# One machine model with turns at SBUF and TensorE's clock windows sets the order of issue of a clustered attention and feed-forward kernel

## The chip, the cores and the metric

The kernel runs on one core of a Trainium2 chip. The metric is device time in microseconds (us). Three runs before the change took 917.51, 917.72 and 917.95 us, a median of 917.72. The profiled execution took 917.96 us. The engines are named as in the profile: PE (TensorE's matmuls), PEld (its weight loads), DVE (VectorE), ACT (ScalarE), POOL (GpSimd) and SP (SyncE, which issues the DMAs).

## The reference

Attention over 4 batches, 8 heads, 768 positions and 64 dimensions, in which a query sees only the keys of its own cluster (of 16); then a feed-forward layer of width 2048 with a piecewise quadratic gate. All is float32.

```python
q_assign = np.argmax(np.einsum('bhsd,hcd->bhsc', q_n, c_n), axis=-1)
k_assign = np.argmax(np.einsum('bhsd,hcd->bhsc', k_n, c_n), axis=-1)
mask = q_assign[:, :, :, None] == k_assign[:, :, None, :]
scores = scale * np.matmul(q, k.transpose(0, 1, 3, 2))
scores = np.where(mask, scores, -1000000000.0)
scores = scores - np.max(scores, axis=-1, keepdims=True)
attn = np.exp(scores)
attn = attn / (np.sum(attn, axis=-1, keepdims=True) + 1e-09)
attn_out = np.matmul(attn, v)
x = attn_out.transpose(0, 2, 1, 3).reshape(B * S, H * D)
h = x @ w_in
g = np.where(h >= 1, h, np.where(h <= -1, 0.0, (h + 1) ** 2 / 4))
out = g @ w_out
```

## The kernel before

Float32 operands are split into a high and a low float16 part, and a product is three matmuls (high by high, high by low, low by high). Heads go in pairs, four pairs in a batch. Queries go in chunks of 256, three chunks in a batch, so there are twelve **units** (a batch and a chunk); for a unit each pair of heads has four score tiles of 128 queries by 768 keys.

A score tile runs so: PE multiplies into a PSUM bank; DVE takes the minimum along a row and copies to SBUF (`sS`, with `sbi`; a custom operation that the order's rows call ISA); ACT takes the exponential; ACT casts the high half (`hl`) and POOL subtracts for the low half; a transposing DMA on SP's queue brings it to `pT`. In the first steps every other tile is transposed on PE instead, ACT casts and DVE subtracts (`pT<-bank`). Then PE multiplies by `v` into `banka`, ACT and DVE scale (`rb`), and ACT and POOL split the result into `x`.

The feed-forward layer of a unit is eight pairs of products. The first product goes into a half bank; DVE clamps (`r`), ACT squares, DVE takes the gate (`r` again), ACT casts (`g`), POOL subtracts, and the second product adds into `bank2`.

The work of preparation lies in the start, and a part of it at each change of batch: for a pair of heads the splits of k and q (`n`, in the first batch also `x`, `g`, `o`) and of v (`kvq<-kvq,sv`), the assignment to clusters (`mx`, `bank`, `has`, `er`) and a product of k by `phi`; a reduction over v (`v_am`); and, once only, sixteen pieces of the weights, each with an absolute value on ACT, a shift on DVE (`wk<-wk`), a merge of bits on DVE (`w<-w,wk`), a sign on ACT, a multiplication on POOL, a scaling and a cast on ACT and a subtraction on POOL (`w<-w`), with small reductions (`w_am`, `w_iw`, `w_sw`). `ffn_scale` makes the scales of the feed-forward layer by sixteen small instructions on DVE.

No engine call issues at once. A `Recorder` keeps each as a node with its engine, its cost in ns (`price`, line 76), what it reads and writes, and the step at which the program asks for it; a group of matmuls is one node. There are 3634. `issue` (line 276) then plans. `forward` goes through time and lets each engine take, from the nodes that are ready, the one of best priority; `backward` does the same from the end and so gives new priorities; after `ROUNDS` the order of the shortest planned span is issued, at one line (291), so all rows of the profile have that line. Each engine runs its instructions in the issued order.

In `price`, a DVE operation of the kind that can wait for POOL at SBUF costs a flat 400 ns more:

```python
wide = [a for a in ins if self.free(a) > 1 or n == 1]
wait = 400 if not ps and (len(wide) > 1 or op in ("tensor_scalar", "tensor_copy")) else 0
```

In `forward`, a matmul costs twice as much before 75 us of planned time (`COLD`) and its plain cost after it.

Of the kernel before, what the change touches and what calls it, by code (L numbers as in the profile page):

```python
# [27 lines left out]


LATENCY = dict(tensor=280, scalar=252, vector=230, gpsimd=175)  # L30
COLD, AHEAD = 75e3, 1500

LOOK, MARGIN = 0.4, 4000
ROUNDS = 8

class Recorder:
# [37 lines left out]
    def price(self, eng, op, out, ins, kw):  # L76

        if "dma" in op:
            n = 1
            for k in out.shape:  # L80
                n *= k
            kb = n * mybir.dt.size(out.dtype) / 1024

            return 33, 79.0 if kb == 2 else kb, "transpose" in op
        n = max(self.free(a) for a in [out] + ins[:1])
        ps = any(a.space == PSUM for a in ins)
        cols = sum(isinstance(kw.get(k), bass.AP) for k in ("scale", "bias", "scalar", "scalar1", "scalar2"))
        if eng == "tensor":
            n = self.free(ins[1])
            half = self.free(ins[0]) <= 64 and n > 100  # L90
            if ins[1].dtype == F32:
                n *= 4

            return n / 4.8 + 9 if half else max(n / 2.4 + 2.5, 24)
        if eng == "scalar":
            cols += kw.get("accum_out") is not None
            first = n == 1 and kw.get("scale") == 0.0
            return 93 + n / 1.2 + 94 * cols - 43 * ps + 1283 * first
        if eng == "vector":
            wide = [a for a in ins if self.free(a) > 1 or n == 1]  # L100
            wait = 400 if not ps and (len(wide) > 1 or op in ("tensor_scalar", "tensor_copy")) else 0
            fast = 1
            if op in ("tensor_scalar", "tensor_copy") and not ps:
                fast = 4 if mybir.dt.size(out.dtype) == 2 and mybir.dt.size(ins[0].dtype) == 2 and n > 64 else 2
            return 68 + n / 0.96 / fast + 61 * cols + 20 * (op == "reciprocal") + wait
        return 55 + n * (2.03 if op == "tensor_tensor" else 0.9 if op == "memset" else 3.5)

    def group(self):
        return Group(self)

    def add(self, eng, op, fn, args, kw):
        outs = [kw[k] for k in ("out", "accum_out") if kw.get(k) is not None]
        pos = [a for a in args if isinstance(a, bass.AP)]
        if "out" not in kw:
            outs.insert(0, pos.pop(0))
        ins = pos + [a for k, a in kw.items() if k not in ("out", "accum_out") and isinstance(a, bass.AP)]
        node = self.open
        if node is None:
            node = Node(eng, self.step, len(self.nodes))
            self.nodes.append(node)  # L120
        assert node.eng == eng
        p = self.price(eng, op, outs[0], ins, kw)
        if isinstance(p, tuple):
            node.cost += p[0]
            node.dma = p[1:]
        else:
            node.cost += p
        node.calls.append((fn, args, kw))
        for aps, w in ((ins, False), (outs, True)):
            for ap in aps:  # L130
                name, parts = self.regions(ap)
                for r in parts:
                    self.touch(node, name, r, w)
                    if ap.space == PSUM:
                        node.banks.update((name, x) for x in range(r[2] // 2048, (r[3] - 1) // 2048 + 1))

    def touch(self, node, name, r, w):
# [12 lines left out]
        keep.append((r, w, node))  # L150
        self.seen[name] = keep

    def forward(self, prio):

        clock, ready, avail = {}, {}, {}
        left = {x: len(x.preds) for x in self.nodes}
        at = dict.fromkeys(self.nodes, 0.0)
        for x in self.nodes:
            if not x.preds:
                heappush(ready.setdefault(x.eng, []), (0.0, prio[x], x.i))  # L160
        hw, ring, sent, span = 450.0, 0.0, [], 0.0
        self.order, bank = [], {}
        todo = len(self.nodes)
        while todo:
            todo -= 1
            best = None
            for e, q in ready.items():
                now = clock.get(e, 0.0)
# [7 lines left out]
            t, e = best  # L176
# [8 lines left out]
            if more:  # L185
# [2 lines left out]
                q.remove((t, prio[self.nodes[i]], i))  # L188
                heapify(q)
                x = self.nodes[i]  # L190

            free = max((until for k in x.banks for o, until in bank.get(k, {}).items() if o != e), default=0.0)
            if free > t:
                clock[e] = t
                heappush(q, (free, prio[x], x.i))
                todo += 1
                continue
            if x.dma and x.dma[0] > 256 and ring > t + AHEAD:

                clock[e] = t  # L200
                heappush(q, (ring - AHEAD, prio[x], x.i))
                todo += 1
                continue
            if x.dma:
                kb, tr = x.dma
                t = max(t, hw, sent[-8] if len(sent) > 7 else 0.0)
                clock[e] = t + x.cost
                hw = t + (650 if tr else 475)
                ring = max(ring, hw + (650 if tr else 784)) + kb * (5.6 if tr else 3.25)
                if tr:  # L210

                    hw = max(hw, ring - 1000)
                end = ring + (400 if tr else 1300)
                sent.append(end)
            else:
                clock[e] = t + x.cost * (2 if e == "tensor" and t < COLD else 1)
                end = clock[e] + LATENCY[e]
            for k in x.banks:
                bank.setdefault(k, {})[e] = end
            x.start, x.busy = t, clock[e]  # L220
            span = max(span, end)
            self.order.append(x)
            for y in x.succs:
                raw = x.dma or x.eng != y.eng or (y.preds[x] and x.eng != "tensor")
                at[y] = max(at[y], end if raw else x.busy)
                left[y] -= 1
                if not left[y]:
                    heappush(ready.setdefault(y.eng, []), (at[y], prio[y], y.i))
        return span

    def backward(self, prio):

# [6 lines left out]
        for _ in self.nodes:  # L239
# [19 lines left out]
                clock[e] = t + kb * (5.6 if tr else 3.25)  # L259
                start[x] = -clock[e] - 1275  # L260
            else:
                clock[e] = t + x.cost
                start[x] = -clock[e]
            for p, raw in x.preds.items():
                lag = 0.0
# [10 lines left out]
    def issue(self):  # L276
# [3 lines left out]
        prio = {x: x.step for x in self.nodes}  # L280
        best = None
        for _ in range(ROUNDS):
            span = self.forward(prio)
            if best is None or span < best[0]:
                best = span, self.order
            prio = self.backward({x: x.start for x in self.nodes})
        span, self.order = best
        with self.tc.manual_schedule():
            for x in self.order:
# [1 line left out]
                    fn(*args, **kw)  # L291


class Node:
    def __init__(self, eng, step, i):
        self.eng, self.step, self.i = eng, step, i
        self.banks = set()
        self.cost, self.dma, self.calls, self.preds, self.succs = 0.0, None, [], {}, []


# [825 lines left out]
```

## Time and profile before

| | |
|---|---|
| Median of three runs | 917.72 us |
| Profiled execution | 917.96 us, span 916.2 us |
| Busy PE, PEld | 819.7, 566.2 us |
| Busy DVE, ACT, POOL | 621.8, 660.5, 580.4 us |
| Mean granted clock of TensorE | 0.961 |
| Idle DVE before a score reduction, for PE | 68.2 us |
| Idle POOL before `hl`, for ACT | 122.1 us |

A row of a group gives line, engine, operation, output and inputs by the program's names, shapes and count; then the busy time, the mean of one in ns, and the idle time of the engine before them with what ended it. A row of a stretch gives its bounds and length, the busy time of each engine with the number of instructions, the granted clock, the share of the DMA engines and GB/s. A row of the timeline gives the start, the duration, and the instruction. A row of waits gives who waited for whom, the sum, the times and the longest.

### The profile page before, as it was taken

The page shows a single profiled execution, that of the slowest core. Times are in us where ns is not written, and L with a number is a line of the kernel's source. Part 1 is how long each engine was busy: PE and PEld are TensorE (multiplying, and loading weights), DVE is VectorE, ACT ScalarE, POOL GpSimd, SP SyncE. Part 2 cuts the span into 40 slices and gives each one's busy share as a digit, 9 for nine tenths or more (in the row PEclk, how much of TensorE's full clock was granted, in tenths as well). Part 3 has the DMA queues.
Part 4 walks back from the last instruction along what each step waited for, and adds up shares of the span by engine and source line. Part 5 has one row for each costly group of instructions (what it writes and reads, how often), then busy time and mean ns, then how long its engine had stood idle before and what let it go on. Part 6 is the DMA issues. An engine that isn't in the chain of part 4 may idle for free.

```text
span 916.2 us, 19559 instructions
## 1 busy us (share of the span) xinstructions
PE 819.7 (89%) x7462; PEld 566.2 (62%) x7462; DVE 621.8 (68%) x1335; ACT 660.5 (72%) x1145; POOL 580.4 (63%) x521
## 2 busy tenths in 40 slices
PE   2556669899998999999998999999998999999998
PEld 2344446556765766776666666666665666667664
DVE  6999987887796665556987665557868555444232
ACT  5778999979767587778676687678766677776232
POOL 1369888986764667766575677656565666666322
PEclk9756779999999999999999999999999999999999
DMA  9989675658998878868899968878998866666100
GB/s 312 238 204 189 133 208 129 152 120 183 185 201 166 161 141 164 156 147 187 166 205 167 176 124 163 157 155 195 178 196 149 149 132 127 111 121 110 30 24 24
DMA packets 403263, 142.82 MB, mean 156 GB/s; under 512 B 380000, under 2 KB 395360, under 8 KB 403168
## 3 DMA queue, kind: packets, MB, share of 16 engines
q1 hardware_dynamic: 403168, 141.56, 76.3%
q8 instruction: 58, 0.95, 0.4%
q14 instruction: 37, 0.30, 0.1%
HBM read 40.40 MB, written 6.29 MB: 51 GB/s over the span
## 4 chain that ended last, share of the span: by engine, by line
PE 68%; DVE 14%; issue 4%; ACT 2%; POOL 2%; ACTq 0%; DVEq 0%; POOLq 0%
PE bank L291 51%; PE banka L291 10%; PE bankh L291 8%; DVE sS L291 3%; DVE r L291 2%; DVE bank L291 2%; DVE kvq L291 2%; DVE n L291 1%; POOL hl L291 1%; DVE w L291 1%; ACT sS L291 1%; DVE mx L291 1%; ACT hl L291 0%; ACT wk L291 0%; DVE bankh L291 0%
## 5 line engine op out<-in xcount | busy, mean ns | idle before, releaser
L291 POOL TENSOR_TENSOR hl<-sS,hl 128x768 f16<-128x768 f32 x181 | 311.4, 1723 | 138.2 <-ACT hl L291 122.1
L291 PE MATMUL bank<-w,g 128*128 128x512 f16 x1152 | 272.7, 380 | 3.0 <-ACT o L291 1.8
L291 PEld LDWEIGHTS <-w 128*128 128x128 f16 x2304 | 223.8, 98 | 62.4 <-issue 21.7
L291 DVE CUSTOM_DVE_ANT_0 sS<-bank,zero,er 128x768 f32<-128x768 f32 x192 | 194.2, 1012 | 88.6 <-PE bank L291 68.2
L291 PEld LDWEIGHTS <-kvq 128*128 128x128 f16 (+1 forms) x3264 | 191.3, 107 | 88.8 <-issue 43.2
L291 ACT ACTIVATE sS<-sS,sbi 128x768 f32<-128x768 f32 x192 | 179.3, 934 | 87.0 <-DVE sbi L291 83.3
L291 PEld LDWEIGHTS <-g 128*128 128x128 f16 x1152 | 111.1, 98 | 120.6 <-POOL g L291 3.3
L291 PE MATMUL bank<-kvq 128*128 128x384 f16 x768 | 163.1, 337 | 17.4 <-DVE sbi L291 7.7
L291 POOL TENSOR_TENSOR g<-r,g 128x512 f16<-128x512 f32 x88 | 104.5, 1187 | 87.3 <-ACT g L291 87.2
L291 ACT CAST hl<-sS 128x768 f16<-128x768 f32 x181 | 148.8, 825 | 3.1 <-DMA pT<-hl 1.7
L291 PE MATMUL bank<-x,w 128*128 128x256 f16 x1056 | 127.9, 274 | 7.2 <-DVE bank L291 3.5
L291 ACT ACTIVATE r<-r,f_ra,f_rs 128x512 f32<-128x512 f32 x88 | 71.3, 810 | 59.0 <-DVE r L291 58.6
L291 PE MATMUL banka<-pT,kvq 128*64 128x256 f16 x1728 | 105.9, 278 | 0.0
L291 DVE TENSOR_SCALAR r<-bank,f_lo,f_hi 128x512 f32<-128x512 f32 x60 | 48.5, 808 | 39.6 <-PE bank L291 32.7
L291 ACT CAST g<-r 128x512 f16<-128x512 f32 x88 | 53.8, 611 | 22.4 <-DVE r L291 13.9
L291 PE MATMUL bank<-wk,w 128*128 128x256 f16 x504 | 60.2, 273 | 4.0 <-DVE bank L291 1.9
L291 POOL TENSOR_TENSOR w<-w 128x1024 f32<-128x1024 f32 (+1 forms) x24 | 52.1, 2177 | 10.6 <-ACT w L291 10.6
L291 PE MATMUL bankh<-x,w 128*128 128x256 f16 x480 | 57.0, 273 | 1.6 <-DVE r L291 1.5
L291 DVE SCALAR_TENSOR_TENSOR r<-bank,f_gs,r 128x512 f32<-128x512 f32 x60 | 44.8, 746 | 13.3 <-ACT r L291 11.3
L291 POOL TENSOR_TENSOR n<-n,phi 128x768 f16<-128x768 f16 x14 | 21.6, 1540 | 28.9 <-DMA kvq<-n 14.9
L291 ACT ACTIVATION_READ_ACCUMULATOR sS<-sS,sbi 128x1 f32 x192 | 36.0, 187 | 0.0
L291 DVE TENSOR_SCALAR r<-bankh,f_lo,f_hi 128x512 f32<-128x512 f32 x28 | 22.6, 809 | 19.5 <-PE bankh L291 16.7
(180 smaller groups left out, 884.0 us busy)
## 6 DMA issues: line engine op xcount, KB each, us to landing
w<-in_moe_w_out_dram SPq DMA_DIRECT2D x14, 512.0 KB, 4.4
kvq<-in_k_dram SPq DMA_DIRECT2D x16, 384.0 KB, 3.8
kvq<-in_q_dram SPq DMA_DIRECT2D x16, 384.0 KB, 3.9
kvq<-in_v_dram SPq DMA_DIRECT2D x16, 384.0 KB, 4.2
out_dram<-o SPq DMA_DIRECT2D x11, 512.0 KB, 3.8
w<-in_moe_w_in_dram SPq DMA_DIRECT2D x10, 512.0 KB, 5.3
n<-in_moe_w_in_dram SPq DMA_DIRECT2D x6, 512.0 KB, 4.2
o<-in_v_dram SPq DMA_DIRECT2D x8, 384.0 KB, 3.9
```

What stands on the lines that cost most here:

```text
L291: fn(*args, **kw)
```

## The change

A class `Machine` replaces what `forward` kept of the state of the engines, and holds two things more. A node is marked `turn` if it is an operation of POOL other than a memset, or one of DVE on two SBUF tensors, or a scalar operation or copy from SBUF to SBUF. Such nodes of the two engines exclude each other in the plan: one starts at the earliest 185 ns (DVE) or 118 ns (POOL) before the end of the last. The flat 400 ns goes; `backward` adds 200 ns to each node that takes a turn, POOL's too. And TensorE's cost goes by windows of 3413 ns: a window is at full pace if the one before held work for over 0.77 of it, or for over 0.41 when it was itself at full pace, and at half pace otherwise. `replay` runs a planned order again with the windows shifted by four phases, and `issue` keeps the order with the least sum of the four spans, of twelve rounds where there were eight. What is computed does not change, nor what each node does.

```diff
-COLD, AHEAD = 75e3, 1500
+AHEAD = 1500
+WINDOW, SLOW, FULL = 3413.0, 0.41, 0.77
+PHASES = (0.0, 850.0, 1700.0, 2550.0)
+TURN, TURN_WAIT = dict(vector=185, gpsimd=118), 200
-ROUNDS = 8
+ROUNDS = 12
...
-            wide = [a for a in ins if self.free(a) > 1 or n == 1]
-            wait = 400 if not ps and (len(wide) > 1 or op in ("tensor_scalar", "tensor_copy")) else 0
...
+    def turns(self, eng, op, out, ins):
+        if eng == "gpsimd":
+            return op != "memset"
+        if eng != "vector" or any(a.space == PSUM for a in ins) or op == "tensor_tensor_reduce":
+            return False
+        wide = [a for a in ins if self.free(a) > 1 or self.free(out) == 1]
+        return len(wide) > 1 or (op in ("tensor_scalar", "tensor_copy") and out.space != PSUM)
...
-                clock[e] = t + x.cost * (2 if e == "tensor" and t < COLD else 1)
-                end = clock[e] + LATENCY[e]
...
+            free = m.free(x, t)
+            if x.dma and x.dma[0] > 256:
+                free = max(free, m.ring - AHEAD)
+            if free > t + 1:
                 clock[e] = t
                 heappush(q, (free, prio[x], x.i))
                 continue
+            end = m.run(x, t)
...
-                clock[e] = t + x.cost
+                clock[e] = t + x.cost + x.turn * TURN_WAIT
...
-            span = self.forward(prio)
+            self.forward(prio)
+            starts = {x: x.start for x in self.nodes}
+            span = sum(self.replay(p) for p in PHASES)
             if best is None or span < best[0]:
                 best = span, self.order
-            prio = self.backward({x: x.start for x in self.nodes})
+            prio = self.backward(starts)
...
+class Machine:
+    def free(self, x, t):
+        for k in x.banks:
+            for e, until in self.bank.get(k, {}).items():
+                if e != x.eng:
+                    t = max(t, until)
+        if x.turn:
+            t = max(t, self.port - TURN[x.eng])
+        return t
...
+            x.busy = self.product(t, x.cost) if e == "tensor" else t + x.cost
+            if x.turn:
+                self.port = x.busy
+            end = x.busy + LATENCY[e]
...
+    def product(self, t, cost):
+        while True:
+            while t >= self.window:
+                self.full = self.work > (SLOW if self.full else FULL) * WINDOW
+                self.window, self.work = self.window + WINDOW, 0.0
+            pace = 1 if self.full else 2
+            part = min(cost * pace, self.window - t)
+            t, self.work, cost = t + part, self.work + part, cost - part / pace
+            if cost < 1e-3:
+                return t
```

The order of issue moves on every engine, by a few places in most of the program and by more in the first quarter. Three places on DVE follow.

The first is some 50 us into the start: preparation of the weights (`w0`, `wk0`) between that of the heads (`kvq`, `g0`). Before:

```order
L291 TENSOR_SCALAR wk0_66<-wk0_66 128x1024
L291 RECIPROCAL sc1_135<-bank2_76 128x2
L291 SCALAR_TENSOR_TENSOR kvq2_63<-kvq2_63,sv0_143 128x768
L291 TENSOR_SCALAR er1_149<-bank2_76,es1_137 128x12
L291 SCALAR_TENSOR_TENSOR g0_71<-kvq3_64,sc1_135,g0_71 128x12x64
L291 SCALAR_TENSOR_TENSOR w0_73<-w0_73,wk0_66 128x1024
L291 TENSOR_REDUCE mx0_146<-bank2_76 128x24
```

At the same place now:

```order
L316 TENSOR_SCALAR wk0_66<-wk0_66 128x1024
L316 TENSOR_SCALAR er1_149<-bank2_76,es1_137 128x12
L316 SCALAR_TENSOR_TENSOR w0_73<-w0_73,wk0_66 128x1024
L316 TENSOR_REDUCE bank1_75<-bank1_75 128x1
L316 RECIPROCAL rs0_160<-rs0_160 128x4
L316 COPY w_am0_0_111<-bank1_75 128x1
L316 TENSOR_SCALAR bank1_75<-bank1_75 128x1
L316 TENSOR_SCALAR bank2_76<-bank2_76 128x1
L316 RECIPROCAL w_sw0_152<-w_iw0_0_119 128x1
L316 TENSOR_SCALAR w_iw0_0_119<-bank1_75 128x1
```

Before, four instructions that take a turn (`wk0`, `kvq2`, `g0`, `w0`) stood within six rows; now the split `g0` comes 15 rows after `w0`, and the split `kvq2` later still.

The second is the multiplication `rb<-banka,rb` for the fourth pair of heads of unit 0, on which the first feed-forward product depends. Before it is row 241 of DVE:

```order
L291 SCALAR_TENSOR_TENSOR w0_73<-w0_73,wk0_66 128x1024
L291 ISA sS1_80,sbi2_158<-bank0_74,zero_105,er0_148 128x768
L291 ISA sbi2_158 128x1
L291 ISA sS2_81,sbi3_159<-bank1_75,zero_105,er0_148 128x768
L291 ISA sbi3_159 128x1
L291 TENSOR_TENSOR rb0_173<-banka_77,rb0_173 128x256
```

Now it is row 252:

```order
L316 TENSOR_REDUCE v_am1_131<-x2_70 128x1
L316 TENSOR_SCALAR wk0_66<-wk0_66 128x1024
L316 TENSOR_REDUCE v_am1_131<-x2_70 128x1
L316 ISA sS2_81,sbi3_159<-bank1_75,zero_105,er0_148 128x768
L316 ISA sbi3_159 128x1
L316 TENSOR_TENSOR pT2_166<-bank0_74,pT2_166 128x6x128
L316 SCALAR_TENSOR_TENSOR w0_73<-w0_73,wk0_66 128x1024
L316 TENSOR_REDUCE bank1_75<-bank1_75 128x1
L316 TENSOR_TENSOR rb0_173<-banka_77,rb0_173 128x256
```

Three reductions `v_am` for the next batch (two of them here) and ten instructions of the first `ffn_scale` have moved ahead of it; one score reduction (`sS1`) has moved behind it.

The third is some 155 us in, with clamps and gates of the feed-forward layer (`r0`) between score reductions. Before:

```order
L291 TENSOR_SCALAR r0_209<-bank1_75,f_lo0_184,f_hi0_179 128x512
L291 ISA sS2_81,sbi1_157<-bank0_74,zero_105,er2_150 128x768
L291 ISA sbi1_157 128x1
L291 RECIPROCAL rs1_161<-rs1_161 128x4
L291 ISA sS0_79,sbi2_158<-bank0_74,zero_105,er2_150 128x768
L291 ISA sbi2_158 128x1
L291 TENSOR_SCALAR wk0_66<-wk0_66 128x1024
L291 SCALAR_TENSOR_TENSOR r0_209<-bank1_75,f_gs0_204,r0_209 128x512
```

Now, from the same clamp:

```order
L316 TENSOR_SCALAR r0_209<-bank1_75,f_lo0_184,f_hi0_179 128x512
L316 TENSOR_SCALAR w_iw0_3_122<-bank1_75 128x1
L316 RECIPROCAL w_sw0_152<-w_iw0_3_122 128x1
L316 TENSOR_TENSOR pT1_165<-bank0_74,pT1_165 128x6x128
L316 SCALAR_TENSOR_TENSOR r0_209<-bank1_75,f_gs0_204,r0_209 128x512
```

Between this clamp and its gate stood two score reductions and a shift of the weights; now there are two small instructions for the weights and the subtraction of a transposed tile.

102 lines of the change are left out of this document (64 added, 38 removed).

## The prediction

> **What bounds the kernel now.** I read first the busy time by stretch, since the page's shares (PE 89%, DVE 68%) are averages over stages with different limits.
>
> ```profile
> core 0: us, PE busy (x) PEld busy (x) DVE busy (x) ACT busy (x) POOL busy (x), PEclk, DMA share, GB/s
> 0.00:23.00 23.00, 5.71 (x83) 4.91 (x83) 15.01 (x37) 13.41 (x23) 4.28 (x27) 1.00 0.94 312
> 23.00:92.00 69.00, 40.12 (x396) 29.49 (x397) 66.81 (x135) 54.02 (x73) 44.61 (x29) 0.65 0.93 210
> 92.00:137.00 45.00, 28.00 (x223) 19.16 (x222) 40.15 (x91) 43.11 (x66) 38.70 (x29) 0.78 0.67 171
> 137.00:206.00 69.00, 61.46 (x529) 41.75 (x528) 55.52 (x163) 61.08 (x106) 60.80 (x50) 0.97 0.61 134
> 206.00:430.00 224.00, 218.16 (x2037) 151.15 (x2035) 153.19 (x329) 167.53 (x305) 146.98 (x131) 1.00 0.85 167
> 430.00:510.00 80.00, 72.80 (x746) 50.11 (x744) 65.59 (x134) 54.54 (x99) 48.89 (x44) 1.00 0.97 178
> 510.00:620.00 110.00, 110.00 (x966) 75.87 (x964) 64.07 (x138) 81.41 (x152) 72.43 (x67) 1.00 0.81 159
> 620.00:710.00 90.00, 81.88 (x837) 56.64 (x836) 72.36 (x145) 64.27 (x115) 56.88 (x50) 1.00 0.97 179
> 710.00:890.00 180.00, 179.98 (x1524) 123.86 (x1523) 82.83 (x162) 114.16 (x204) 102.23 (x95) 1.00 0.55 102
> 890.00:916.20 26.20, 21.61 (x138) 13.23 (x136) 6.24 (x8) 6.99 (x10) 4.62 (x4) 0.99 0.06 21
> ```
>
> From 206 us on the bound is PE: 510 to 620 and 710 to 890 have 0.02 us of idle PE in 290. No order of issue gains there, since every order runs the same matmuls. Time can come from four places: the start up to 206, where PE is idle for 206 - 135.3 = 70.7 us; the middle of 206 to 430 (5.8 idle); the two changes of batch (7.2 and 8.1); the last 26 (4.6), where ACT and POOL keep their order. In the start it is not PE that ends last. From 23 to 92 DVE is busy for 66.81 of 69, from 92 to 137 ACT for 43.11 of 45, and from 137 to 206 ACT and POOL for 61 of 69 each. The view of waits says the same from PE's side, for 23 to 137:
>
> ```profile
> PE bank L291 <- ACT sS L291: 22.2, 10, 5.8
> PE bank L291 <- DVE bank L291: 13.2, 5, 4.0
> ```
>
> PE waits there for scores that have been through DVE and then ACT, and for a PSUM bank that DVE still reads.
>
> **The change, part by part.** It removes and adds no instruction; all 3634 recorded steps are issued in another order. So the whole effect is in waits, and I price the kinds of wait that the new planner can see.
>
> *Turns of DVE and POOL at SBUF.* An instruction of DVE on two SBUF tensors, or a copy or scalar operation from SBUF to SBUF, shows a long duration when POOL is at work. First the groups of such instructions between 23 and 137 us, with busy time, mean of one and idle time before; then single ones from the timeline.
>
> ```profile
> L291 DVE SCALAR_TENSOR_TENSOR w<-w,wk 128x1024 uint32<-128x1024 uint32 x11 | 23.1, 2098 | 0.0
> L291 DVE TENSOR_SCALAR wk<-wk 128x1024 uint32<-128x1024 uint32 x11 | 12.5, 1135 | 2.3 <-ACT wk L291 2.2
> L291 DVE SCALAR_TENSOR_TENSOR kvq<-kvq,sv 128x768 f16<-128x768 f32 x4 | 4.9, 1237 | 0.0
> L291 DVE TENSOR_SCALAR kvq<-kvq,phi 128x1536 f16<-128x1536 f16 x3 | 4.0, 1323 | 0.0
> L291 DVE SCALAR_TENSOR_TENSOR g<-kvq,sc,g 128x768 f16<-128x768 f32 x1 | 2.2, 2233 | 0.0
> ```
>
> ```profile
> 29.49 1.22 DVE L291 SCALAR_TENSOR_TENSOR w<-w,wk 128x1024 uint32<-128x1024 uint32 x1
> 42.52 0.68 DVE L291 TENSOR_SCALAR wk<-wk 128x1024 uint32<-128x1024 uint32 x1
> 45.08 0.61 DVE L291 TENSOR_SCALAR kvq<-kvq,phi 128x1536 f16<-128x1536 f16 x1
> 52.45 1.00 DVE L291 SCALAR_TENSOR_TENSOR kvq<-kvq,sv 128x768 f16<-128x768 f32 x1
> 55.69 2.91 DVE L291 SCALAR_TENSOR_TENSOR w<-w,wk 128x1024 uint32<-128x1024 uint32 x1
> ```
>
> The same sign merge takes 1.22 us at 29.49, with POOL idle, and 2.91 at 55.69. The wait inside the durations is 11 x (2.098 - 1.22) = 9.7 for the merges, 11 x (1.135 - 0.68) = 5.0 for the shifts, 3 x (1.323 - 0.61) = 2.1 for the products with phi, 2.2 - 1.0 = 1.2 and 4 x (1.237 - 1.00) = 0.9 for the splits: 19 us of DVE's 107 in the stretch where DVE or what hangs on it is last. Bounds of what the order saves: nothing, if turns fall as they did, and at most ACT's idle time, 114 - 54.0 - 43.1 = 16.9, since ACT is late next. The trace cannot say which share goes. The order says something: of 34 such DVE instructions in this part 13 stood within three places of the one before, and 10 of 35 do now. That is a quarter fewer pairs; the new planner also sees POOL's side. I take a third, 6 us.
>
> *What now stands ahead of the first feed-forward product.* It needs the fourth pair of heads of unit 0. The kinds of DVE instruction that this concerns:
>
> ```profile
> L291 DVE CUSTOM_DVE_ANT_0 sS<-bank,zero,er 128x768 f32<-128x768 f32 x22 | 22.0, 1009 | 1.9 <-PE bank L291 1.9
> L291 DVE TENSOR_REDUCE v_am<-x 128x1 bf16<-128x768 f32 x2 | 1.9, 936 | 0.0
> L291 DVE TENSOR_SCALAR f_inv<-bankh,isx 128x2 f32<-128x2 f32 x1 | 0.2, 220 | 0.0
> L291 DVE TENSOR_SCALAR bank<-bank 128x1 f32<-128x1 f32 x13 | 2.1, 167 | 0.0
> ```
>
> Ahead of DVE's multiply for that pair (rb<-banka,rb) stand 13 more instructions than before: three reductions over v (3 x 0.94 = 2.8), ten of feed-forward scales and one of a weight's maximum (of the sizes of the last two rows, 1.8 together), and one score reduction of 1.0 less: 3.6 us more. On POOL it is 1.7 more, one product of weights (1.89, below) less two tiny copies. By unit 1's fourth pair the queue ahead is as long as before (-0.6 us), so this is a delay that is given back, if PE's backlog lasts over it. I charge 2 of the 3.6, because PE idles in 137 to 206 for only 7.5 us and so already has other work there. The start gives -6 + 2 = -4.
>
> *Feed-forward ahead of scores.* Between 150 and 200 us PE's queue now has feed-forward groups up to 6 places earlier and score groups up to 6 places later. Each is work that PE does anyway; 7.5 us of idle PE bound a gain there. A loss is bounded by the second rival below. I take nothing.
>
> *The changes of batch.* The same waits, from the same kind of row:
>
> ```profile
> L291 DVE SCALAR_TENSOR_TENSOR n<-kvq,sc,n 128x768 f16<-128x768 f32 x6 | 7.7, 1304 | 0.1
> L291 DVE SCALAR_TENSOR_TENSOR kvq<-kvq,sv 128x768 f16<-128x768 f32 x4 | 7.5, 1882 | 0.0
> L291 DVE TENSOR_SCALAR kvq<-kvq,phi 128x1536 f16<-128x1536 f16 x4 | 3.6, 898 | 0.0
> ```
>
> For 430 to 510 that is 6 x 0.30 + 4 x 0.88 + 4 x 0.29 = 6.5 us. A third of it, 2 us, is saved by DVE, which is busy for 66 of 80; PE is idle for 9% there and gets perhaps a quarter of it. Twice 0.5 is -1; bounds are all of PE's idle time (-15.3 in both) and as much again as a loss if pairs of heads come later; I take the value nearest to the rows, -1.
>
> *TensorE's clock.* The new planner counts work in windows. PE's 40.1 and 28.0 us at 0.65 and 0.78 would be 26.1 and 21.8 at full clock, 20 us less; at half clock 52 and 44, 28 us more. PE idles for 46 us in that stretch and waits for others, so I charge 0 either way; if PE's transposes are last, up to a few us appear on either side.
>
> *SP's queue.* Transposing DMAs and loads move by up to 20 places. The DMA share is 0.93 from 23 to 92 us, but POOL's one long wait for a DMA in the start stands ahead of this instruction, and the first eight of POOL's steps are the same in both orders. I take nothing.
>
> ```profile
> 32.37 1.49 POOL L291 TENSOR_TENSOR n<-n,phi 128x768 f16<-128x768 f16 x1 [13.39 <-DMA kvq<-n]
> ```
>
>
> Sum: -4 - 1 = -5 against the profiled execution's own 917.96 (its span of 916.2 and 1.8 around it), which gives 913.0. That execution is 0.24 above the median of 917.72, within what these runs scatter.
>
> **The rivals.**
>
> *The turns are full, so the waits only change sides: 918.* This is also the case in which the change doesn't do what it says. POOL is busy for 44.6 + 38.7 = 83.3 us of the 114 from 23 to 137. DVE's instructions of the turn kind need, without waiting, 11 x 1.22 + 11 x 0.68 + 3 x 0.61 + about 11 x 1.0 = 34 us. Together that is 117 of 114. POOL's 83 hold waits of its own. The group hl in the start and again from 510 to 610 us, then two groups of weights in the start and single ones of these from the timeline:
>
> ```profile
> L291 POOL TENSOR_TENSOR hl<-sS,hl 128x768 f16<-128x768 f32 x10 | 20.9, 2093 | 9.9 <-ACT hl L291 9.9
> L291 POOL TENSOR_TENSOR hl<-sS,hl 128x768 f16<-128x768 f32 x29 | 47.7, 1646 | 19.6 <-ACT hl L291 16.1 <-DVE r L291 1.8 <-ACT rs L291 1.1
> ```
>
> ```profile
> L291 POOL TENSOR_TENSOR w<-w 128x1024 f16<-128x1024 f32 x9 | 21.3, 2362 | 8.3 <-ACT w L291 8.3
> L291 POOL TENSOR_TENSOR w<-w 128x1024 f32<-128x1024 f32 x10 | 20.8, 2079 | 1.1 <-ACT w L291 1.1
> ...
> 101.45 2.13 POOL L291 TENSOR_TENSOR w<-w 128x1024 f16<-128x1024 f32 x1
> ...
> 105.48 1.89 POOL L291 TENSOR_TENSOR w<-w 128x1024 f32<-128x1024 f32 x1
> ```
>
> That is 10 x (2.09 - 1.65) = 4.5 us for hl, and 9 x 0.23 + 10 x 0.19 = 4.0 for the weights. Without them the two engines need some 109 of 114. So little is free that an order can hardly part them; what DVE saves POOL would wait. Then nothing is saved at the turns or at the batches, and the time stays at 918, or within 2 us of it if the first product is late. Against it: POOL is idle for 69 - 44.6 = 24 us before 92 us, 13.4 of them in the wait above. The Trainium skill, page "SBUF — State Buffer", section "SBUF: two separate sides", says that the pair of ports which DVE and GpSimd share is an exclusive lock: who starts first holds it for the whole instruction and the other blocks. By that rule a new order gains only where the loser had something else to do, and with both queues full the time would be this rival's 918; the trace's 2.91 against 1.22 agrees that the wait is a full one, not a slowing. Chance 0.21.
>
> *The scores come late and PE runs dry: 922.* Feed-forward scales, weights and clamps now stand ahead of unit 1's third pair of heads: 29 more instructions on DVE (two score reductions of 1.0, a clamp of 0.8 and a gate of 0.75, four steps of weights of 0.4 to 1.2, and 21 small ones of about 0.16: some 9.6 us), and the three reductions ahead of unit 0's fourth. If the turns save DVE less than 3.6 us, the first feed-forward product is late by the rest, and if PE's backlog of unit 0 ends before unit 1 is ready, PE idles for what it lacks. The price is the full 3.6 with nothing saved, and about 1 at the changes of batch: 917.96 + 4 = 922. It decides as soon as DVE's saving falls under 3.6. For it: DVE is the full engine of 23 to 92. Against it: by unit 1's fourth pair nothing is left of the delay. Chance 0.23.
>
> **How the numbers follow.** My forecast, 913, with all its sizes from 2 to 14 us less, has 0.56. Its far end is half of the 19 us saved, nothing charged for the first product, and 4 us at the batches: 904. The other end of the range is the slower rival, 922. Measurements of this kernel can tell about 0.2% (1.8 us) from no change, so the three cases are at the same time the chances of faster, same and slower: 0.56, 0.21, 0.23.
>
> **What would show it.** Before, the first feed-forward group starts here:
>
> ```profile
> 134.83 4.08 PE L291 MATMUL bank<-x,w 128*128 128x256 f16 x24
> ```
>
> In the profile after, the merges w<-w,wk of the start fall from 2098 ns to some 1800 and the shifts from 1135 to some 980 (the first step); POOL's mean of hl in the start does not rise over 2093 (the first rival, if it does); this first group starts some 2 to 4 us earlier (the start); idle PE in 137 to 206 stays under 8 us (the second rival, if it grows); idle PE at the two changes of batch falls from 15.3 to about 14. The prediction is wrong if DVE's durations fall and the end does not move: then ACT, at 43.11 of 45, took the gain.

## The result and the profile after

| | before | after |
|---|---|---|
| Median | 917.84 us (4 runs, 917.51 to 918.73) | 933.61 us (4 runs, 932.52 to 934.68) |
| Ratio, 95% interval | | 1.017 (1.0153 to 1.0188) |
| Profiled execution, span | 917.96, 916.2 us | 932.73, 930.9 us |
| Busy PE | 819.7 us | 823.3 us |

The change makes the kernel 15.8 us slower. 913.0 was forecast with 904 to 922 as the range, so the forecast was wrong in its sign and the range did not hold the time.

Busy time by stretch of the kernel after (columns as in the prediction: bounds, length, then PE, PEld, DVE, ACT, POOL with their instructions, granted clock, DMA share, GB/s):

```profile
23.00:92.00 69.00, 39.67 (x403) 29.24 (x403) 64.71 (x145) 48.72 (x71) 36.38 (x27) 0.88 0.87 192
92.00:137.00 45.00, 26.39 (x192) 18.07 (x191) 36.36 (x79) 42.06 (x59) 39.88 (x27) 0.73 0.66 196
137.00:206.00 69.00, 60.66 (x539) 43.10 (x540) 56.40 (x149) 61.04 (x106) 58.14 (x49) 0.98 0.62 127
206.00:430.00 224.00, 212.51 (x1947) 145.73 (x1945) 148.51 (x332) 163.85 (x300) 145.62 (x132) 0.98 0.85 166
430.00:510.00 80.00, 75.50 (x795) 53.15 (x793) 60.29 (x126) 55.33 (x99) 48.41 (x43) 1.00 0.92 175
620.00:710.00 90.00, 81.73 (x803) 55.97 (x802) 65.62 (x138) 62.81 (x113) 50.30 (x45) 1.00 0.91 170
```

In 23 to 137 us every engine that could be last is busy for less time, though the stretch is as long. Idle DVE rises from 114 - 66.81 - 40.15 = 7.0 to 114 - 64.71 - 36.36 = 12.9 us, idle ACT from 16.9 to 23.2, idle POOL from 30.7 to 37.7. In 206 to 430, which the prediction took for nothing, idle PE rises from 5.8 to 11.5. But stretches fixed in time do not hold the same work in the two kernels, so where the time went is better read from equal work: points at which PE has issued exactly the same groups of matmuls in both, and the same group stands last. Such groups in PE's timeline of before (L291) and after (L316), start and duration:

```profile
119.54 1.54 PE L291 MATMUL bank<-idf,sS 128*128 128x128 f32 x6 [2.29 <-ACT sS L291]
228.45 0.41 PE L291 MATMUL banka<-idu,rr 128*64 128x128 f16 x8
280.34 0.81 PE L291 MATMUL bank<-kvq 128*128 128x384 f16 x4 [0.63 <-DVE sbi L291]
370.05 1.46 PE L291 MATMUL bank<-w,g 128*128 128x512 f16 x6
558.58 0.81 PE L291 MATMUL bank<-kvq 128*128 128x384 f16 x4
740.94 0.41 PE L291 MATMUL banka<-idu,rr 128*64 128x128 f16 x8
```

```profile
128.73 1.54 PE L316 MATMUL bank<-idf,sS 128*128 128x128 f32 x6 [2.27 <-ACT sS L316]
233.14 0.41 PE L316 MATMUL banka<-idu,rr 128*64 128x128 f16 x8
293.27 0.81 PE L316 MATMUL bank<-kvq 128*128 128x384 f16 x4
378.63 2.75 PE L316 MATMUL bank<-w,g 128*128 128x512 f16 x12
571.06 0.82 PE L316 MATMUL bank<-kvq 128*128 128x384 f16 x4
754.82 0.41 PE L316 MATMUL banka<-idu,rr 128*64 128x128 f16 x8
```

The lag of after is 128.73 - 119.54 = 9.2 us at the 66th of the 728 groups, 4.7 at the 148th, 293.27 - 280.34 = 12.9 at the 195th, 381.38 - 371.51 = 9.9 (the ends) at the 271st, 12.5 at the 434th, 13.9 at the 592nd and 930.9 - 916.2 = 14.7 at the end. So the start costs 4.7, the stretch between 230 and 370 us 5.2, the change of batch after 430 us 2.6, the one after 620 us 1.4, and the tail 0.8. No single place holds the whole loss, but one loses most at a stroke: the first change of batch. There the lag grows from 5.7 us at the 178th group to 12.9 at the 195th; 3.0 of it are given back by the 271st. The rows from the start of the 178th group to that of the 195th, of before and of after:

```profile
258.80:280.34 21.54, 18.54 (x195) 12.68 (x194) 19.09 (x38) 12.46 (x23) 16.28 (x14) 1.00 0.97 185
```

```profile
264.45:293.27 28.82, 21.40 (x196) 13.81 (x194) 21.06 (x47) 14.31 (x25) 13.57 (x12) 0.88 0.69 139
```

The same groups take 28.82 us in place of 21.54. PE is idle for 7.4 us in place of 3.0, most of it in two waits for DVE (2.81 and 3.21 us, below), and busy for 21.40 in place of 18.54: 2.9 of the 7.3 us are the same matmuls running longer, with the granted clock at 0.88 in place of 1.00.

**The turns shrank, as much as forecast in sum and not row by row.** DVE's groups between 23 and 137 us of after, and POOL's group `hl`:

```profile
L316 DVE SCALAR_TENSOR_TENSOR w<-w,wk 128x1024 uint32<-128x1024 uint32 x10 | 14.9, 1493 | 0.0
L316 DVE TENSOR_SCALAR wk<-wk 128x1024 uint32<-128x1024 uint32 x11 | 13.2, 1204 | 2.7 <-ACT wk L316 2.7
L316 DVE SCALAR_TENSOR_TENSOR kvq<-kvq,sv 128x768 f16<-128x768 f32 x4 | 5.9, 1484 | 0.0
L316 DVE TENSOR_SCALAR kvq<-kvq,phi 128x1536 f16<-128x1536 f16 x3 | 3.6, 1211 | 0.0
L316 DVE SCALAR_TENSOR_TENSOR g<-kvq,sc,g 128x768 f16<-128x768 f32 x1 | 1.0, 1009 | 0.0
```

```profile
L316 POOL TENSOR_TENSOR hl<-sS,hl 128x768 f16<-128x768 f32 x10 | 18.1, 1809 | 4.1 <-ACT hl L316 2.3 <-DMA kvq<-x 1.8
```

Over the same shortest durations as in the prediction the waits inside them are now 10 x (1.493 - 1.22) = 2.7, 11 x (1.204 - 0.68) = 5.8, 4 x (1.484 - 1.00) = 1.9, 3 x (1.211 - 0.61) = 1.8 and 0.0: 12.2 us against 19, so 6.7 us saved, where a third, 6, was forecast. 0.9 of the 6.7 is only that the stretch holds ten merges in place of eleven. The merges fell by more than forecast (1493 ns, forecast 1800), the shifts rose (1204 ns from 1135, forecast 980), and so did the splits of v (1484 from 1237): the size of the sum is in part luck. POOL's `hl` fell too. Over the whole program, where both kernels do the same work, DVE's busy time fell from 621.8 to 613.2 us and POOL's from 580.4 to 572.7. The saving did not arrive at the end. In the stretch DVE's idle time grew by 5.9, which is the same number as its smaller busy time (107.0 to 101.1), since the stretch is as long. Who waited, in the views of waits of 23 to 137 us, first three rows of before, then of after (sum, times, longest):

```profile
POOL w L291 <- ACT w L291: 9.4, 6, 5.2
ACT sS L291 <- DVE sbi L291: 5.4, 10, 2.0
PE bank L291 <- DVE wk L291: 3.2, 2, 3.0
```

```profile
POOL w L316 <- ACT w L316: 25.9, 7, 6.7
ACT sS L316 <- DVE sbi L316: 7.7, 4, 3.7
ACT bankh L316 <- DVE has L316: 3.2, 1, 3.2
PE bank L316 <- DVE wk L316: 9.3, 4, 7.7
PE bank L316 <- ACT sS L316: 12.5, 7, 3.9
```

Waits between engines have grown: POOL for ACT, ACT for DVE, PE for DVE's shifts. Others have shrunk, PE for `sS` from 22.2 to 12.5 and PE for `bank` from 13.2 to 3.9; in all PE is idle for 47.9 us of the 114 in place of 45.9. That the time saved inside durations turned into just these waits is likely and not shown. The first feed-forward product, forecast 2 to 4 us earlier than 134.83, came 5.4 later:

```profile
140.19 2.60 PE L316 MATMUL bankh<-x,w 128*128 128x256 f16 x12
```

### The profile page after: what moved, and what is told of

Its sections match the earlier page's. It is cut to its first block, busy times and chain, and to the rows that moved or that the text cites. A ratio compares the mean times of both kernels' runs of the same rounds, so it can differ in the third digit from the quotient of the medians.

```text
span 930.9 us, 19523 instructions
## 1 busy us (share of the span) xinstructions
PE 823.3 (88%) x7462; PEld 568.7 (61%) x7462; DVE 613.2 (66%) x1335; ACT 658.5 (71%) x1145; POOL 572.7 (62%) x521
## 4 chain that ended last, share of the span: by engine, by line
PE 66%; DVE 12%; ACT 3%; issue 2%; DMA 1%; POOL 0%; ACTq 0%; DVEq 0%
PE bank L316 48%; PE banka L316 9%; PE bankh L316 8%; DVE sS L316 3%; DVE r L316 3%; DVE bank L316 2%; DVE n L316 1%; DVE kvq L316 1%; ACT sS L316 1%; DVE mx L316 1%; ACT r L316 1%; DMA pT<-hl 1%; DVE bankh L316 1%; ACT hl L316 1%; ACT w L316 0%
## 5 line engine op out<-in xcount | busy, mean ns | idle before, releaser
L316 POOL TENSOR_TENSOR hl<-sS,hl 128x768 f16<-128x768 f32 x181 | 304.2, 1686 | 151.9 <-ACT hl L316 129.8
L316 PE MATMUL bank<-w,g 128*128 128x512 f16 x1152 | 269.8, 379 | 4.4 <-ACT o L316 3.0
L316 PEld LDWEIGHTS <-w 128*128 128x128 f16 x2304 | 225.2, 98 | 69.9 <-issue 29.0
L316 DVE CUSTOM_DVE_ANT_0 sS<-bank,zero,er 128x768 f32<-128x768 f32 x192 | 194.0, 1011 | 83.1 <-PE bank L316 69.2
L316 PEld LDWEIGHTS <-kvq 128*64 128x64 f16 (+1 forms) x3264 | 192.4, 107 | 90.1 <-issue 43.7
L316 ACT ACTIVATE sS<-sS,sbi 128x768 f32<-128x768 f32 x192 | 179.0, 932 | 88.4 <-DVE sbi L316 86.5
L316 PEld LDWEIGHTS <-g 128*128 128x128 f16 x1152 | 110.9, 98 | 121.7 <-issue 5.0
L316 PE MATMUL bank<-kvq 128*128 128x384 f16 x768 | 163.5, 338 | 18.9 <-DVE sbi L316 9.2
L316 POOL TENSOR_TENSOR g<-r,g 128x512 f16<-128x512 f32 x88 | 104.3, 1185 | 88.3 <-ACT g L316 80.9
L316 ACT CAST hl<-sS 128x768 f16<-128x768 f32 x181 | 148.2, 826 | 7.1 <-DMA pT<-hl 5.7
L316 PE MATMUL bank<-x,w 128*128 128x256 f16 x1056 | 128.2, 274 | 14.5 <-DVE r L316 3.6
L316 ACT ACTIVATE r<-r,f_ra,f_rs 128x512 f32<-128x512 f32 x88 | 71.3, 811 | 68.7 <-DVE r L316 68.2
L316 PE MATMUL banka<-pT,kvq 128*64 128x256 f16 x1728 | 107.0, 280 | 0.0
L316 DVE TENSOR_SCALAR r<-bank,f_lo,f_hi 128x512 f32<-128x512 f32 x60 | 48.4, 807 | 43.0 <-PE bank L316 35.2
L316 POOL TENSOR_TENSOR w<-w 128x1024 f32<-128x1024 f32 (+1 forms) x24 | 51.1, 2136 | 29.1 <-ACT w L316 27.3
L316 ACT CAST g<-r 128x512 f16<-128x512 f32 x88 | 53.7, 611 | 16.2 <-DVE r L316 11.1
L316 PE MATMUL bank<-wk,w 128*128 128x256 f16 x504 | 60.4, 272 | 4.8 <-DVE bank L316 3.3
L316 PE MATMUL bankh<-x,w 128*128 128x256 f16 x480 | 59.5, 279 | 1.0 <-DVE er L316 0.7
L316 DVE SCALAR_TENSOR_TENSOR r<-bank,f_gs,r 128x512 f32<-128x512 f32 x60 | 44.9, 749 | 21.8 <-ACT r L316 15.5
L316 PEld LDWEIGHTS <-ones 128*128 128x128 bf16 x244 | 17.9, 110 | 34.7 <-issue 25.1
L316 DVE TENSOR_SCALAR r<-bankh,f_lo,f_hi 128x512 f32<-128x512 f32 x28 | 22.6, 808 | 23.6 <-PE bankh L316 15.0
L316 POOL TENSOR_TENSOR n<-n,phi 128x768 f16<-128x768 f16 x14 | 22.0, 1569 | 23.8 <-DVE phi L316 12.1
```

## The experiments

All compare with the kernel before on the same chip; its medians there were 917.75 to 918.97 us. Lags are taken at equal work against the trace of before, as above. Theory P, which the profile suggested: the loss arises at a few places where the new order makes an engine wait. Its rivals came up as the runs went on.

**One model at a time.** In the first run the windows of TensorE's clock go, in the second the turns, in the third both, so that only the new search is left.

```diff
 class Machine: def product(self, t, cost):        # turn_only, neither
-        while True:
...
+        return t + cost * (2 if t < 75e3 else 1)
 def price / def turns                              # clock_only, neither
+            wide = [a for a in ins if self.free(a) > 1 or n == 1]
+            wait = 400 if not ps and (len(wide) > 1 or op in ("tensor_scalar", "tensor_copy")) else 0
-            return 68 + n / 0.96 / fast + 61 * cols + 20 * (op == "reciprocal")
+            return 68 + n / 0.96 / fast + 61 * cols + 20 * (op == "reciprocal") + wait
...
+        return False
```

> The planner of after with its model of turns at SBUF, but without the windows of TensorE's clock: matmuls cost twice as much before 75 us and their plain price behind it, as in before. Theory P (places): the loss comes from where the turns' prices move work on DVE, ACT and POOL, in the start and at the first change of batch, and the clock model has nothing to do with it: 926 to 934 us, with the merges w<-w,wk of the start at 1400 to 1700 ns as in after. Rival C (clock): the windows of the clock put the work in wrong places, and without them the turns do their work: 912 to 919 us. Rival N (the search): any new search among orders ends some 10 us worse, whatever the costs: 926 to 934 here and also in the run with neither model.

> The planner of after with the windows of TensorE's clock, but with before's flat 400 ns on DVE's SBUF instructions in place of the turns. Theory P (places by the turns' prices): 914 to 921 us, as before, and merges w<-w,wk of the start back at 1900 to 2200 ns. Rival C (clock): 926 to 934 us. Rival N (the search): 926 to 934 us.

> The search of after (12 rounds, the order chosen by the sum of four replays) with before's costs in both places: flat 400 ns on DVE, matmuls twice as dear before 75 us. Theories P and C: within 4 us of before, 914 to 922 us. Rival N (the search): 926 us or more.

Measured: the turns alone 921.59 us (ratio 1.004, 1.0025 to 1.0055), the windows alone 931.3 (1.015, 1.0134 to 1.0167), neither 920.48 (1.0027, 1.0015 to 1.0039). P as put there, with the turns to blame, falls, and so does rival N in that form. It looked like rival C: the windows of the clock cost 11 to 12 us (931.3 against 920.48, 933.61 against 921.59); but the turns alone, 921.59, lay above C's 912 to 919 too. Each was one order only. And for N the third run says little: with before's costs the new search walks through the same eight orders as the old one and then issues its tenth.

The merges between 23 and 137 us took 1379 ns on average with the turns alone (forecast 1400 to 1700), 1780 with the windows alone (forecast 1900 to 2200), and in `neither`:

```profile
L313 DVE SCALAR_TENSOR_TENSOR w<-w,wk 128x1024 uint32<-128x1024 uint32 x11 | 17.0, 1543 | 0.1
```

That is nearly after's 1493, with before's flat 400 ns, so short merges alone do not show the model of turns at work. Over the whole program it does seem to spare DVE some time: the eight orders planned with turns (all runs, here and below) keep DVE busy for 603 to 615 us, median 609.6, the eight without for 610 to 622, median 619.9. The end does not follow: those eight with turns take between 921.6 and 935.3 us.

**After's start alone.** The order is written out as a list of steps: all that before issues up to the 155th group in after's relative order, the rest as before.

```diff
-        span, self.order = best
+        self.order = [self.nodes[i] for i in ORDER]
```

> Before's order with one stretch replaced: all that before issues up to the 155th group of matmuls (near 236 us) stands in after's relative order, all behind it in before's order. At the same 155 groups after was 4.7 us late. Theory P, losses stay where they arise and add up: 917.8 + 4.7, so 921 to 924 us. Rival S (slack): the later stretches wait for something else and take the lag up: 917 to 919 us. Rival J: the loss is one of the whole order, so that a piece of it alone does as much as all: above 928 us.

Measured: 922.49 us (1.005, 1.0033 to 1.0067), where theory P put it. The lag is 3.3 us at the 148th group and 4.3 from the 185th to the end: the start's loss stays where it arises, and nothing later takes it up. After was 4.7 late at the 148th group with the same order up to there, so 1.4 us is what two executions of one start can differ by.

**Other rounds of the same planners.** The planner makes one order per round and issues the one that it rates best. Fewer rounds, with no other edit, give another order from the same costs.

```diff
-ROUNDS = 12
+ROUNDS = 8        # after_8; 6 in after_6; 5 in clock_5; before_6: 6 in place of 8
```

> The kernel after with 8 rounds of its search in place of 12, and nothing else: the order comes from another round of the same planner with the same costs. Theory C (the windows of TensorE's clock cost some 12 us, as the runs with one model each suggest): 928 to 937 us, like after. Rival D (draw: rounds of one planner differ on the chip by as much as the change does, and the planner's ranking among them says little): away from 933.6 by over 4 us, most likely 918 to 928 us, since 917.8, 920.5 and 921.6 were seen from three other settings.

> The kernel after with 6 rounds of its search: a third round of the same planner and costs. Theory C: 928 to 937 us. Rival D: 918 to 935 us, and over 4 us away from at least one of the other two rounds of the same planner.

> The kernel before with 6 rounds of its search in place of 8: another round of the old planner with the old costs. Theory C: 915 to 921 us, since the old costs make good orders. Rival D: the round that before took was a lucky one, and this one is slower by over 4 us: 922 to 932 us.

> The run with the windows of the clock and the flat 400 ns, 931.3 us, with 5 rounds of its search in place of 12: another round, same costs. Theory C: 927 to 935 us. Rival D: away from 931.3 by over 4 us, most likely 918 to 927 us.

Measured: 922.45 us (1.005, 1.003 to 1.007), 932.52 (1.0168, 1.0148 to 1.0188), 932.58 (1.0162, 1.0142 to 1.0182) and 933.84 (1.0168, 1.0145 to 1.0192). `after_6` and `clock_5` lie where theory C put them, `after_8` and `before_6` do not; `before_6` decides most: the old planner with the old costs gives 932.58 from another round, as slow as the change, and the new planner gives 922.45. The 932.58 loses at no one place either: its lags are 4.0 at the 153rd group, 4.4 at the 264th, 11.5 at the 441st and 14.9 at the 592nd.

**Single places of after, and an order in pieces.** In `ffn_late` the first feed-forward scale (3 steps of ACT, 16 of DVE) stands later; in `n_first` two one-hot copies of DVE stand ahead of two splits; `turn_8` is another round with the turns alone; `pieced` joins stretches of three orders.

```diff
-  ACT bankh<-w_am, bankh<-w_iw x2; DVE bankh<-bankh,isx ... f_rs    (near 81 to 98 us)
+  the same 19 steps behind DVE sS<-bank,zero,er of 141 us           (ffn_late)
-  DVE n<-kvq,sc,n x2, n<-bank x2
+  DVE n<-bank x2, n<-kvq,sc,n x2                                    (n_first)
```

> An order put together from three that have run, cut where TensorE has done the same groups in each: up to the 204th group the relative order of the run with neither model (3.4 us ahead of before there), then before's, from the 513th to the 574th group that of the run with the turns alone (it gains 5.1 us on before between these two points), and before's to the end. Theory D (each order is a sum of stretches that turned out well or badly, and lags stay where they arise): 917.8 - 3.4 - 5.1, so 908 to 911 us. Rival S (a stretch's gain hangs on what stood ahead of it, so that pieces of different orders don't fit): 915 us or more.

> The order of after with one group moved back: the first feed-forward scale's 3 copies on ACT (which waited 3.25 us at 81.4 us with ACT's queue behind them) and its 16 instructions on DVE stand behind the score reduction at 141 us, about where before has them; nothing else moves. Theory P (this wait and the DVE work make the start's lag): the lag of 9.2 us at the 66th group falls to 5 to 6 us, and the end comes 2 to 3.5 us earlier, 930 to 931.6 us. Rival S (another chain ends last there, since another order has the group as early without a wait): the end moves by less than 1 us, 932.6 to 934.6 us.

> The order of after with two instructions moved: the two one-hot copies n<-bank of DVE at 271.9 us, for which TensorE waits 2.81 us, stand ahead of the two splits n<-kvq,sc,n (1.01 and 2.47 us) instead of behind them; nothing else moves. Theory P: the 2.81 us gap goes to under 0.8 us and the end comes 1.5 to 2.8 us earlier, 930.8 to 932.1 us. Rival S (the gap behind it, 3.21 us at 285.8, is set by the same late DVE and grows by as much): the end moves by less than 1 us.

> The run with the turns alone (921.6 us) with 8 rounds of its search in place of 12: another round, same costs. Theory D (draw): anywhere from 917 to 935 us, over 4 us away from 921.6 with a chance of a half. Theory C (only the windows of the clock make orders slow): 918 to 925 us.

Measured: `ffn_late` 935.43 us (1.018, 1.0166 to 1.0194) and `n_first` 933.2 (1.0163, 1.0142 to 1.0185). Both intervals overlap that of after, so neither gains, and P falls for both places, in a way worth seeing (rival S holds for `n_first`; `ffn_late` ended even above its band). In `n_first` PE's wait went, and another came at the next group (PE's timeline of after, then of `n_first`):

```profile
272.26 0.32 PE L316 MATMUL bankh<-n,ones 128*128 128x32 f16 x6 [2.81 <-DVE n L316]
272.86 2.72 PE L316 MATMUL bankh<-x,w 128*128 128x256 f16 x12 [0.28 <-DVE has L316]
285.76 2.67 PE L316 MATMUL bank<-x,w 128*128 128x256 f16 x12 [3.21 <-DVE mx L316]
```

```profile
267.95 0.30 PE L284 MATMUL bankh<-n,ones 128*128 128x32 f16 x6
271.48 1.98 PE L284 MATMUL bankh<-x,w 128*128 128x256 f16 x12 [3.23 <-DVE has L284]
284.80 1.66 PE L284 MATMUL bank<-x,w 128*128 128x256 f16 x12 [3.22 <-DVE mx L284]
```

2.81 + 0.28 became 3.23: the splits, moved behind, now delay `has`. In `ffn_late` the 66th group comes 3.3 us earlier than in after, as P forecast, and the 77th 1.3 later. About half of the 3.3 is not the move: `start_new` and `n_first`, with after's own order up to there, have the 66th group 1.4 and 1.8 us earlier than after. DVE's timeline of `ffn_late` (first and last of the moved steps, and what stands behind them), and PE's:

```profile
139.86 0.23 DVE L284 TENSOR_SCALAR bankh<-bankh,isx 128x2 f32<-128x2 f32 x1 [0.40 <-ACT bankh L284]
...
142.79 0.15 DVE L284 SCALAR_TENSOR_TENSOR f_rs<-bankh,f_inv 128x2 f32<-128x2 f32 x1
142.86 0.95 DVE L284 TENSOR_TENSOR pT<-bank,pT 128x768 f16<-128x768 f32 x1
```

```profile
143.86 0.81 PE L284 MATMUL bank<-kvq 128*128 128x384 f16 x4 [2.87 <-DVE pT L284]
```

The moved steps take DVE 142.86 - 139.86 = 3.0 us, `pT` is that much later, and PE waits 2.87 us for it. In these two places a step that went back on DVE only made another one late.

`pieced` took 915.11 us (0.997, 0.9958 to 0.9982): faster than before by 0.3%, but not by the 0.9% of theory D, and where rival S put it. The first piece brought 2.1 us at its end in place of 3.4, and of the 3.5 that the second gained by the 574th group 2.6 went by the 589th. `turn_8` took 930.6 us (1.0138, 1.0097 to 1.018), 9 us from the other round with the same costs; its four runs lie between 926.0 and 937.3.

**Costs or draw.** What was left open was whether the new costs make slower orders on the whole. Here one round is issued, whatever the planner thinks of it.

```diff
-            if best is None or span < best[0]:
+            if True:                                # the last of ROUNDS rounds
```

> Before's planner and costs; the order of its 5th round is issued, whatever the planner thinks of it. Theory D (draw: the rounds of either planner scatter over the same 918 to 936 us): anywhere in there. Theory C (the new costs make slower orders on the whole): 917 to 925 us, so that before_6 with 932.6 was the exception among the old ones.

> Before's planner and costs, the order of its 6th round. Theory D: anywhere from 918 to 936 us. Theory C: 917 to 925 us.

> Before's planner and costs, the order of its 8th round (before itself is the 7th). Theory D: anywhere from 918 to 936 us. Theory C: 917 to 925 us.

> After's planner and costs, the order of its 5th round. Theory D: anywhere from 918 to 936 us. Theory C: 928 to 937 us, so that after_8 with 922.5 was the exception among the new ones.

> After's planner and costs, the order of its 10th round. Theory D (draw): anywhere from 918 to 936 us. Theory C (the new costs make slower orders on the whole): 928 to 937 us.

> After's planner and costs, the order of its 12th and last round (after itself is the 11th). Theory D: anywhere from 918 to 936 us. Theory C: 928 to 937 us.

All orders that planners chose or made, medians in us:

| costs | round and median |
|---|---|
| before's | 3rd 932.6 (`before_6`), 5th 930.1, 6th 918.4, 7th 917.8 (before), 8th 920.5 |
| before's, new search | 10th 920.5 (`neither`) |
| turns alone | 921.6 (12 rounds), 930.6 (8 rounds) |
| windows alone | 931.3 (12 rounds), 933.8 (5 rounds) |
| both, after's | 5th 935.3, 6th 932.5, 8th 922.5, 10th 925.4, 11th 933.6 (after), 12th 932.5 |

The intervals of the last six runs against before: `before_r5` 1.0126 (1.008 to 1.0171), `before_r6` 1.0007 (0.9997 to 1.0017), `before_r8` 1.0034 (1.0015 to 1.0052), `after_r5` 1.0196 (1.0148 to 1.0243), `after_r10` 1.0075 (1.0055 to 1.0094), `after_r12` 1.0145 (1.0121 to 1.0168).

Shown is that the round alone is worth 14.8 us with the old costs and 12.9 with the new ones, nearly as much as the change itself, and that before stands on the best old order that was run (the 6th round, at 1.0007, is as good). Theory C in its plain form falls: two of six old orders (the 10th counted) are as slow as most new ones, two of six new ones are faster than these. A weaker form stays possible: the eight orders made with the clock's windows have a median of 932.5 us, the eight without 921.1, and only three of the latter are over 930. The rounds of one search start from one another, so these are not sixteen independent draws, and the question is left open. Why such orders should be slower was not found.

The planners do not see the difference. The old one puts its 3rd and 6th rounds at 898.6 and 898.8 us of planned time, and they took 932.6 and 918.4; the new one puts its 8th and 11th at 899.3 and 898.4 (a quarter of its sum of four spans), and they took 922.5 and 933.6.

## Why the prediction was wrong

- **The turns.** The sum came out: 6.7 us of waits gone against 6, though not by the rows that were to show it (the shifts were to fall to 980 ns and rose to 1204), and orders made without the model of turns have merges nearly as short (1530 ns in `before_6`, 1543 in `neither`, against 1493). Wrong was the next step, to enter the 6 in the sum as time of the end: the start came 4.7 us later. The text named the sign of this ("wrong if DVE's durations fall and the end does not move") and the wrong taker: ACT did not take the gain as a full engine, since its own idle time grew by 6.3. DVE, ACT and POOL all idle more in 23 to 137 us.
- **What stands ahead of the first product.** Charged with 2 us of 3.6; the first group came 5.4 late. The start gave +4.7 in place of -4, 8.7 of the 19.7 us between forecast and result (-5 against +14.7 by spans). `start_new` shows that this part stands by itself. The prediction charged only DVE's queue here (it named 1.7 us on POOL and left them out); the waits of after name ACT's and POOL's too.
- **The middle.** 206 to 430 us was listed among the places where time can come from and then got no term: 0 in the sum, and in no rival. This is the step that failed most plainly. 5.2 us went between 230 and 370 us: the first change of batch alone took 7.3, of which 3.0 came back. The prediction speaks of "the two changes of batch"; four batches have three, and the first, near 270 us, lay hidden in the middle with 5.8 us of idle PE. That idle time bounds what an order can gain there; it does not bound what an order can lose.
- **The changes of batch.** -1 was taken for the two that were counted and 2.6 + 1.4 = +4.0 came, inside the bounds of 15.3 either way that the text gave. These bounds were then not carried to the range, which ended at 922. By equal work the lag even grows to 16.8 us at the 514th group, inside the last change, and falls back.
- **TensorE's clock.** Taken at 0. For the start nothing here speaks against that. At the first change of batch it does not hold: 2.9 of the 7.3 us are the same matmuls at a granted clock of 0.88, and over the whole program PE is busy for 823.3 us in place of 819.7. As a cost in the planner the clock may have moved the result by its choice of order, which is open.
- **The rivals.** Against the first (turns full) stands POOL's `hl`, 1809 ns against 2093, and POOL's smaller busy time. The second had the right sign, but its place was wrong: DVE saved more than the 3.6 from which it was to decide, idle PE in 137 to 206 grew only from 7.5 to 8.3 us, and its price, 4, is under a third of what came.
- **Behind all of it** is the sentence "I price the kinds of wait that the new planner can see". All 3634 steps were ordered anew, and what such an order costs beyond these waits is not seen by either planner: two orders from one set of costs differ by up to 15 us. One order from each planner could not show which planner is better.

## What to carry to other kernels

When a change replaces a searched order, first measure other orders of the same search: their scatter is the uncertainty of any forecast for it, to both sides, and a gain in one kind of wait that is smaller than the scatter cannot be foreseen. A stretch in which the bound engine is nearly always busy has little room to gain, but its idle time does not bound what can be lost there. A wait removed in an engine that others wait for is a gain only once the trace shows that nobody's idle time has grown by as much.

## What the runs showed of the hardware

The granted clock of a row has to be read beside the durations of the matmuls. After and `start_new` issue the same relative order in the start. The row of 23 to 92 us of `start_new` (that of after stands above), then the row of 23 to 46 us and four products of 128x384, of after and of `start_new`:

```profile
23.00:92.00 69.00, 39.93 (x405) 29.36 (x405) 64.74 (x148) 50.01 (x72) 36.29 (x28) 0.61 0.89 200
```

```profile
23.00:46.00 23.00, 13.90 (x124) 9.71 (x124) 21.06 (x44) 13.51 (x20) 6.00 (x4) 1.00 0.71 189
39.16 1.44 PE L316 MATMUL bank<-kvq 128*128 128x384 f16 x4 [1.61 <-DVE sbi L316]
```

```profile
23.00:46.00 23.00, 15.20 (x129) 10.83 (x129) 21.06 (x48) 14.43 (x21) 5.63 (x4) 0.50 0.79 199
37.86 1.44 PE L284 MATMUL bank<-kvq 128*128 128x384 f16 x4 [1.61 <-DVE sbi L284]
```

From 23 to 46 us the clock reads 1.00 in the one and 0.50 in the other, and the same products take 1.44 us in both; from the 17th to the 158th group the two traces stay within 1.2 to 1.4 us of each other. So after's 0.88 for 23 to 92 us is not the clock that its matmuls had: the records of the clock in its trace begin only at 60.6 us (in `start_new` at 15.0), and a stretch without a record counts as 1.00. The Trainium skill, page "TensorE: Matmul & The Clock Gate", section "Seeing it yourself", warns that clock events in a trace have been seen to be unreliable; after's row of 23 to 46 us agrees with it.

Where the records are there, the durations go with them. The four products that took 1.44 us take 0.81 in after at 293.27 us (above). And at the first change of batch, behind the idle time of 2.81 us, twelve matmuls of 128x256 take 2.72 us at 272.86 (above), in this row, and 1.47 seven microseconds later:

```profile
272.00:276.00 4.00, 3.46 (x23) 2.48 (x23) 3.52 (x11) 1.46 (x3) 1.44 (x1) 0.57 0.98 182
279.82 1.47 PE L316 MATMUL bank<-x,w 128*128 128x256 f16 x12
```
